# SwiGLU's token groups in the order second, third, first, with the first group's products by seven for eight

## The chip, the cores and the metric

The kernel runs on one core of a Trainium2 chip. The metric is the time of one execution on the device in microseconds; of several runs the median counts. The profile is one further execution, recorded by the hardware profiler, with its own time.

## What is computed

Attention with softmax on q (over the head dimension) and on k (over the sequence), an expert layer in which every expert is applied to all 2304 tokens and weighted by a matrix P (eight rounds of row and column normalization), and a SwiGLU layer with an RMS norm ahead of it:

```python
x = attn_out.transpose(0, 2, 1, 3).reshape(2304, 512)
# experts: P from exp(x @ w_gate), 8 rounds
for e in range(8):
    out += P[:, e:e + 1] * (np.maximum(x @ w1[e], 0.0) @ w2[e])   # 512 -> 1024 -> 512
# SwiGLU on x = out
xn = x / sqrt(mean(x * x) + 1e-06) * rms_g
g = xn @ w_gate                                                  # 512 -> 1536
return (g * sigmoid(g) * (xn @ w_val)) @ w_out
```

## The kernel before

**Precision.** Every operand of a large product is split into a high and a low part (`split`, L100); `mm3` (L104) issues three matmuls for one product: high by high, high by low, low by high. In the trace these are lines 105, 106 and 107.

**Groups and units.** The tokens are in three groups of 512, 896 and 896 tokens; `GP` (L55) holds half of these, 256, 448 and 448. Features of the hidden layers are taken 256 at a time (`CH`). One such chunk for one group is a unit: 32 units a group in the expert layer (units 0 to 95, `NU` is 96), six a group in SwiGLU (`NC2` is 6, units 96 to 113). Each unit has a part h, which computes the hidden features, and a part y, which multiplies them with the second weights and adds to the group's sum, one 128-token tile after another: four tiles in group 0, seven in the others, six matmuls of 512 columns for each tile.

**Two ways of h.** `plain` (L845) multiplies directly: 24 matmuls of 512 columns for group 0. `seven` (L793) takes the product as two by two blocks and makes it from seven block products instead of eight (`PROD`, L788): 42 matmuls whose columns are one half of the group's tokens, 448. It needs sums and differences of the weight blocks (stored to DRAM ahead, loaded by `ws_load`, L287) and of the token blocks (seven tiles `SX`, named B11, T1, B21, T2, B22, T4, T3, built in 36 steps by `sx_all`, stored in DRAM, loaded by `sx_load`, L739). The seven products go to three PSUM places b1, b2, b3, of which b1 alone has two buffers. After each product something reads it out: ScalarE copies (`keep`, L800, line 802 in the trace) after products 1, 2, 4 and 7, VectorE adds after 3, 5 and 7 (lines 816, 820, 825), GpSimd adds after 7 (line 826). Group 0 goes by `plain` in both layers, the others by `seven`.

**SwiGLU.** `unit2_h` (L1040) makes the gate product a, applies the sigmoid on ScalarE (L1046) and multiplies on VectorE (L1047), then makes the value product v, multiplies (L1050), and splits the result for y (L1052, L1053). In the groups by seven the a pass and the v pass follow each other directly: 84 matmuls. The second weights are split in task places 4 and 5 of the a pass (`w2_split`), after which the next ones are requested.

**Order.** `stretch` (L1141) writes out the order of the parts on TensorE: within a stretch h of the next unit comes ahead of y of the unit before, and a new stretch begins with h, h, y. Three calls make: expert groups 0 and 1; expert group 2 with SwiGLU groups 0 and 1; SwiGLU group 2. The side work is hung by `task` and `spread` (L1242) on numbered places within h and y, one step a place; each engine runs its instructions in the order issued. All transfers are issued by SyncE (SP) in order. `norm_steps` (L1029) makes the RMS norm of a group: sums of squares on ScalarE (L953), a root (L957), scaling on VectorE (L974), transposes on TensorE with copies on ScalarE (L1020), and the `sx_all` steps. For group 0 it ends instead in `norm_first` (L978), which stores the normed tokens in `XN0D`; `first_again` (L996) loads them for SwiGLU.

Of the kernel before, what the change touches and what calls it, by code (L numbers as in the profile page):

```python
# [8 lines left out]
F32 = mybir.dt.float32  # L9
# [9 lines left out]
def kernel(  # L19
# [23 lines left out]
    nc = tc.nc  # L43
# [26 lines left out]
    EPS = 1e-9  # L70
    LATE = 4

    const = ctx.enter_context(tc.tile_pool(name="const", bufs=1))
# [213 lines left out]
    def ws_load(key):  # L287

        ws_alloc(key)
        for w, t in zip("hl", WS[key]):  # L290
            t = t.rearrange("p a k f -> p (a k f)").bitcast(F32)
            if key[1] < NU:
                nc.sync.dma_start(t, WSD[key + (w,)])
            else:
                g, c = divmod(key[1] - NU, NC2)
                d = WSD[key[0], c, w]
                if g:
                    nc.sync.dma_start(t, d[:, 2 * P:])
                else:
                    nc.sync.dma_start(t[:, :8 * P], d[:, :8 * P])  # L300

# [434 lines left out]
    def sx_alloc(nm, g):  # L736
        SX[nm] = sxp.tile([P, 2, 2, G], F32R, tag=nm, name=f"s{nm}_{g}")

    def sx_load(g, i):  # L739
        nm = NAMES[i]  # L740
        sx_alloc(nm, g)
        nc.sync.dma_start(SX[nm].rearrange("p w j n -> p (w j n)").bitcast(F32), SXD[nm, g])

    def sx_steps(g, j, b11, b21, b12, b22, stored):

        shp = b11.shape[1:]

        v = (lambda t: t.rearrange("p (a n) -> p a n", a=shp[0])) if len(shp) > 1 \
            else (lambda t: t)

        def put(nm, s):
            if stored:
                if j == 0:
                    SXD[nm, g] = dram.tile(
                        [P, 4 * G], F32, tag=f"{nm}{g}", name=f"sd{nm}_{g}"
                    )
                d = SXD[nm, g].rearrange("p (w j n) -> p w j n", w=2, j=2)
                return list(halves(
                    f"{nm}_{g}_{j}", s, lambda t: v(t[:, :G]), lambda w: v(d[:, w, j]),
                    None if g == NG + 2 else staged,  # L760
                ))
# [15 lines left out]

# [15 lines left out]
    def seven(key, c, hook, after):  # L793

        wh, wl = WS.pop(key)
        nm = f"{key[0]}_{key[1]}"
        bk = {}
        tmp = {}

        def keep(n, i):  # L800
            tmp[n] = cp_.tile([P, G], F32, tag="u1" if n == "u3" else n, name=f"{n}_{nm}")
            nc.scalar.copy(tmp[n], bk[i])  # L802

        for i, (w, x, b, first) in enumerate(PROD):
            if first:
                bk[b] = pb_tile(f"b{b}", f"b{b}_{nm}_{i}")[:, :G]
            s = SX[x]
# [25 lines left out]
    def group(u):  # L833
        return (u // NCH, u % NCH) if u < NU else divmod(u - NU, NC2)

# [8 lines left out]

    def plain(u, f, key, stored):  # L845

        ph = bank("h", 2 * GP[0], f"ph_{key[0]}_{u}_{f}")
        plain_mm(ph, f, key, stored, range(KD))
        return ph

    def plain_mm(ph, f, key, stored, kks):
        wh, wl = WS[key]
        xh, xl = X0
        for kk in kks:
            if stored:
                i = ((2, 3), (0, 1))[f][kk // 2]
                lh, ll = wh[:, i, kk % 2], wl[:, i, kk % 2]
            else:
                lh, ll = (plain_view(t)[:, kk, f * P:(f + 1) * P] for t in (wh, wl))
            mm3(ph, lh, ll, xh[:, kk], xl[:, kk], kk == 0, kk == KD - 1)  # L860
# [9 lines left out]
    def unit_h(u, hook):  # L870
        if u < NCH:
            hook(0)
            for f in range(2):
                if f:
                    hook(1)
                if u == 0:
                    ph = FIRST_PH[f]
                    plain_mm(ph, f, ("a", 0), False, (KD - 1,))
                else:
                    ph = plain(u, f, ("a", u), False)  # L880
                relu(*h_tiles(u, f), ph)()
            del WS["a", u]
            hook(2)
            return
# [90 lines left out]

    XN0D = {}

    def norm_first(kk):  # L978

        pn = bank("y", DM, f"pn_0_{kk}")  # L980
        for t in range(TPG[0]):
            nc.tensor.transpose(
                pn[:, t * P:(t + 1) * P], ACC[0, 0][:, t, kk * P:(kk + 1) * P], ident
            )
        hi, lo = piece(f"xn0_{kk}")
        nc.scalar.activation(hi, pn, AF.Copy, scale=rmsg[:, kk:kk + 1])
        nc.vector.scalar_tensor_tensor(
            lo, pn, rmsg[:, kk:kk + 1], hi.bitcast(F32), op0=ALU.mult, op1=ALU.subtract
        )
        if kk == 0:  # L990
            XN0D[0] = dram.tile([P, 2 * KD * DM], F32, tag="xn0", name="xn0")
        d = XN0D[0].rearrange("p (w k n) -> p w k n", w=2, k=KD)
        for w, t in enumerate((hi, lo)):
            nc.sync.dma_start(d[:, w, kk], t.bitcast(F32))

    def first_again():  # L996
        nonlocal X0
        t = slot_a()
        nc.sync.dma_start(t.bitcast(F32), XN0D[0])
        X0 = as_x0(t)  # L1000

    def norm_place(g, kk, h):
# [3 lines left out]
    def norm_transpose(g, kk):  # L1006
        n = TPG[g]
        per = P // 2
        pns = []
        for i in range(2):  # L1010
            pn = bank("y", DM, f"pn_{g}_{kk}_{i}")
# [12 lines left out]

        out_(0, 0, n, pns[0][:, :n * per])
        out_(1, 0, 8 - n, pns[0][:, n * per:])
# [13 lines left out]
    def unit2_h(u, hook):  # L1040
# [15 lines left out]

        cg = cp_.tile([P, 2, 2, G], F32, tag="c", name=f"cg_{u}")
        if g == 0:
            for f in range(2):
                hook(f)  # L1060
                to = cg[:, f].rearrange("p t g -> p (t g)")[:, :n]
                gate_part(plain(u, f, ("a", u), True), to, f)
            del WS["a", u]
            hook(2)
            for f in range(2):
                hook(3 + f)
                to = cg[:, f].rearrange("p t g -> p (t g)")[:, :n]
                value_part(plain(u, f, ("v", u), True), to, f)()
            del WS["v", u]
            hook(5)  # L1070
            return
        flat = lambda t, f: t[:, f].rearrange("p t g -> p (t g)")
        cv = cp2.tile([P, 2, 2, G], F32, tag="cv", name=f"cv_{u}")
        hook(-1)
# [72 lines left out]
    stretch(0, 2 * NCH)  # L1147
    stretch(2 * NCH, NCH + 2 * NC2)
    stretch(NU + 2 * NC2, NC2)

# [27 lines left out]
    for n, key in enumerate(keys):  # L1178
# [4 lines left out]
        i = 6 if kd == "a" else 13  # L1183
        if u >= NU and group(u)[0] == 0:
            i = 2 if kd == "a" else 5
        task("h", u, i, lambda key=key: ws_load(key))
# [101 lines left out]
    for i in range(7):  # L1288
        task("h", NU + 2 * NC2 - 1, 7 + i, lambda i=i: sx_load(NG + 2, i))

    with tc.manual_schedule():
# [52 lines left out]
        def first_h(i):  # L1344
            if i == 0:
                FIRST_PH.extend(bank("h", 2 * GP[0], f"ph_a_0_{f}") for f in range(2))
            for f in range(2):
                plain_mm(FIRST_PH[f], f, ("a", 0), False, (i,))

# [147 lines left out]
```

## Time and profile before

| | |
|---|---|
| median of 3 runs | 2025.71 us (2025.29 to 2025.9) |
| the profiled execution | 2025.36 us, span 2023.6 us |
| TensorE busy | 1999.9 us, 99% |
| VectorE busy | 1408.3 us, 70% |
| ScalarE busy | 782.7 us, 39% |
| GpSimd busy | 412.5 us, 20% |
| DMA | 415.09 MB, mean 205 GB/s |
| share of TensorE in the chain that ended last | 95% |

Busy time of TensorE counts a matmul from its start to its modelled end; consecutive matmuls overlap in the records, so the rate of work is read from the number of matmuls in a stretch, not from the mean duration of one. Idle time of an engine that is not the bottleneck costs nothing.

### The profile page before, as it was taken

To read this page: it belongs to the slowest core of one execution; us is meant where nothing else is said; L and a number is where in the kernel's file an instruction comes from. 1 tells how busy PE (TensorE), PEld (TensorE's weight loads), DVE (VectorE), ACT (ScalarE), POOL (GpSimd) and SP (SyncE) were. 2 spreads that over 40 slices of the span, in tenths; PEclk is the share of its full clock that TensorE was granted. 3 is DMA by queue.
4 is the path that set the end of the run, shared out by engine and by line. 5 is a ranking of instruction groups with operands and counts; after the bars stand their busy time and mean duration, and the time that the engine had idled before them with its cause. 6 is when DMAs were issued, how large, how long until landed. Compare 5 with 4: busy or idle time off the path is not lost.

```text
span 2023.6 us, 25473 instructions
## 1 busy us (share of the span) xinstructions
PE 1999.9 (99%) x9454; PEld 1727.4 (85%) x9454; DVE 1408.3 (70%) x2161; ACT 782.7 (39%) x1383; POOL 412.5 (20%) x388
## 2 busy tenths in 40 slices
PE   7999999999999999999999999999999999999999
PEld 5887888888888888888888888888888888888887
DVE  8785877776767777777658878878865446565555
ACT  5554333345433434433243333333332243432432
POOL 5551000031222222222013222222220000110100
PEclk9999999999999999999999999999999999999999
DMA  7443223355755566554777778878865647657542
GB/s 205 132 138 105 94 95 99 99 186 183 263 202 203 210 220 219 205 201 176 292 268 267 258 246 313 278 264 291 281 235 189 263 144 262 217 203 271 195 159 75
DMA packets 154236, 415.09 MB, mean 205 GB/s; under 512 B 13568, under 2 KB 66304, under 8 KB 153728
## 3 DMA queue, kind: packets, MB, share of 16 engines
q1 hardware_dynamic: 154112, 413.47, 58.6%
q8 instruction: 74, 1.21, 0.2%
q14 instruction: 50, 0.41, 0.1%
HBM read 281.69 MB, written 131.73 MB: 204 GB/s over the span
## 4 chain that ended last, share of the span: by engine, by line
PE 95%; DVE 3%; DMA 1%; ACT 0%; issue 0%; POOL 0%; SPq 0%; DVEq 0%; POOLq 0%; ACTq 0%
PE py L105 13%; PE py L106 13%; PE py L107 13%; PE b_a L107 10%; PE b_a L106 10%; PE b_a L105 10%; PE ph_a L105 3%; PE ph_a L107 3%; PE ph_a L106 3%; PE po L107 2%; PE po L105 2%; PE po L106 2%; PE b_v L105 2%; PE b_v L107 2%; PE b_v L106 2%; PE pv L573 1%
## 5 line engine op out<-in xcount | busy, mean ns | idle before, releaser
L105 PE MATMUL py<-w2h,hh 128*128 128x512 f32 x1152 | 452.7, 393 | 0.7 <-ACT lt L685 0.7
L106 PE MATMUL py<-w2l,hh 128*128 128x512 f32 x1152 | 449.0, 390 | 0.0
L107 PE MATMUL py<-w2h,hl 128*128 128x512 f32 x1152 | 448.6, 389 | 0.0
L802 ACT COPY u_a<-b_a 128x448 f32<-128x448 f32 x228 | 121.6, 533 | 693.6 <-PE b_a L107 693.4
L105 PEld LDWEIGHTS py<-w2h,hh 128*128 128x128 f32 x1152 | 216.2, 188 | 47.2 <-issue 1.5
L107 PEld LDWEIGHTS py<-w2h,hl 128*128 128x128 f32 x1152 | 216.3, 188 | 45.7
L106 PEld LDWEIGHTS py<-w2l,hh 128*128 128x128 f32 x1152 | 216.4, 188 | 43.0
L105 PE MATMUL b_a<-sT,wsh_a 128*128 128x448 f32 x608 | 220.1, 362 | 3.3 <-DVE c L816 2.1
L107 PE MATMUL b_a<-sT,wsl_a 128*128 128x448 f32 x608 | 220.7, 363 | 0.0
L106 PE MATMUL b_a<-sT,wsh_a 128*128 128x448 f32 x608 | 220.3, 362 | 0.0
L930 DVE SCALAR_TENSOR_TENSOR slot_a<-py,Pm,slot_a 128x512 f32<-128x512 f32 x217 | 162.5, 749 | 52.4 <-PE py L107 50.3
L930 DVE SCALAR_TENSOR_TENSOR slot_b<-py,Pm,slot_b 128x512 f32<-128x512 f32 x217 | 161.1, 745 | 23.5 <-PE py L107 22.5
L107 PE MATMUL b_a<-sB,wsl_a 128*128 128x448 f32 x456 | 165.7, 363 | 0.1
L106 PE MATMUL b_a<-sB,wsh_a 128*128 128x448 f32 x456 | 165.2, 362 | 0.0
L105 PE MATMUL b_a<-sB,wsh_a 128*128 128x448 f32 x456 | 165.2, 362 | 0.0
L102 DVE TENSOR_TENSOR w2l<-w2r,w2h 128x512 fp32r<-128x512 f32 x162 | 118.2, 730 | 43.6 <-ACT w2h L101 43.6
L826 POOL TENSOR_TENSOR c<-u_a,p_a 128x448 f32<-128x448 f32 x64 | 73.9, 1155 | 344.3 <-ACT u_a L802 344.2
L864 DVE SCALAR_TENSOR_TENSOR hl<-c,hh 128x896 fp32r<-128x896 f32 x128 | 143.1, 1118 | 0.9 <-ACT hh L863 0.7
L247 POOL TENSOR_TENSOR sum<-w1r 128x256 f32<-128x256 f32 x32 | 23.7, 741 | 562.2 <-DMA w1r<-in_moe_w_dram 244.2
L863 ACT ACTIVATE hh<-c 128x896 fp32r<-128x896 f32 x128 | 122.3, 956 | 27.9 <-POOL c L826 27.9
L101 ACT CAST w2h<-w2r 128x512 fp32r<-128x512 f32 x162 | 97.1, 618 | 81.4 <-PE py L107 77.0
L105 PEld LDWEIGHTS b_a<-sT,wsh_a 128*128 128x128 f32 x608 | 113.7, 187 | 13.2 <-DVE c L816 3.7
(236 smaller groups left out, 3654.6 us busy)
## 6 DMA issues: line engine op xcount, KB each, us to landing
w2r<-in_moe_w_dram SPq DMA_DIRECT2D x96, 512.0 KB, 4.6
w1r<-in_moe_w_dram SPq DMA_DIRECT2D x64, 512.0 KB, 3.4
wsdh<-wsh_a SPq DMA_DIRECT2D x32, 896.0 KB, 6.6
wsdl<-wsl_a SPq DMA_DIRECT2D x32, 896.0 KB, 7.9
wsh_a<-wsdh SPq DMA_DIRECT2D x32, 896.0 KB, 6.5
wsl_a<-wsdl SPq DMA_DIRECT2D x32, 896.0 KB, 8.5
w2d<-w2l SPq DMA_DIRECT2D x32, 512.0 KB, 2.9
w2l<-w2d SPq DMA_DIRECT2D x32, 512.0 KB, 4.8
```

Of the source, the lines that this page charges most:

```text
L101: nc.scalar.copy(hi, src)
L102: (eng or nc.vector).tensor_tensor(lo, src, hi.bitcast(F32), op=ALU.subtract)
L105: nc.tensor.matmul(ps, lh, rh, start=first, stop=False, skip_group_check=True)
L106: nc.tensor.matmul(ps, lh, rl, start=False, stop=False, skip_group_check=True)
L107: nc.tensor.matmul(ps, ll, rh, start=False, stop=last, skip_group_check=True)
L247: nc.gpsimd.tensor_tensor(s1, a21, a22, op=ALU.add)
L573: nc.tensor.matmul(st["pv"][:, :P], st["ke"][:, c].rearrange("p h d -> p (h d)"), st["v"][:, :, c, :], start=(c == 0), stop=(c == SC - 1),)
L802: nc.scalar.copy(tmp[n], bk[i])
L826: nc.gpsimd.tensor_tensor(c[:, 1, 1], tmp["u3"], tmp["p5"], op=ALU.add)
L863: nc.scalar.activation(th, src, AF.Relu)
L864: return lambda: nc.vector.scalar_tensor_tensor(tl, src, 0.0, th.bitcast(F32), op0=ALU.max, op1=ALU.subtract)
L930: nc.vector.scalar_tensor_tensor(a, py, pe, a, op0=ALU.mult, op1=ALU.add)
```

## The change

SwiGLU's groups come in the order 1, 2, 0 (`TURN2`), and each has a stretch of its own. Group 0's unit goes by `seven` as the others', with block columns of 256 tokens, so an h of SwiGLU has 84 matmuls in every group. Group 0's norm ends in transposes and the 36 `sx_all` steps, with DRAM tiles of its own; `norm_first`, `XN0D` and `first_again` go. The norm of group 0 has more places (units 33 to 38, h and y), the `sx_all` of expert group 2 begins two units later, the norm of group 2 lies in five units of SwiGLU group 1 (ten places in h, three in y), and the SX tiles of the three groups are loaded during the last h of the group ahead of each. Weight blocks are loaded at the same places in all groups: 14 of 16 blocks for group 0 too, where it had 8.

```diff
+    TURN2 = (1, 2, 0)
 def ws_load(key):
-                if g:
-                    nc.sync.dma_start(t, d[:, 2 * P:])
-                else:
-                    nc.sync.dma_start(t[:, :8 * P], d[:, :8 * P])
+                nc.sync.dma_start(t, d[:, 2 * P:])
 def sx_alloc(nm, g):
-        SX[nm] = sxp.tile([P, 2, 2, G], F32R, tag=nm, name=f"s{nm}_{g}")
+        w = GP[g % NG]
+        t = sxp.tile([P, 4 * G], F32R, tag=nm, name=f"s{nm}_{g}")[:, :4 * w]
+        SX[nm] = t.rearrange("p (w j n) -> p w j n", w=2, j=2)
 def seven(key, c, hook, after):
+        w_ = GP[group(key[1])[0]]
-                bk[b] = pb_tile(f"b{b}", f"b{b}_{nm}_{i}")[:, :G]
+                bk[b] = pb_tile(f"b{b}", f"b{b}_{nm}_{i}")[:, :w_]
 def group(u):
+        j, c = divmod(u - NU, NC2)
+        return TURN2[j], c
 def norm_steps(g):
-        if g == 0:
-            return steps + [lambda kk=kk: norm_first(kk) for kk in range(KD)]
 def unit2_h(u, hook):
-        if g == 0:
-            for f in range(2):
-                hook(f)
-                gate_part(plain(u, f, ("a", u), True), to, f)
-            for f in range(2):
-                hook(3 + f)
-                value_part(plain(u, f, ("v", u), True), to, f)()
-            return
 ...
-    stretch(2 * NCH, NCH + 2 * NC2)
-    stretch(NU + 2 * NC2, NC2)
+    stretch(2 * NCH, NCH)
+    for j in range(NG):
+        stretch(NU + j * NC2, NC2)
 ...
-            task("h", u, (0 if group(u)[0] == 0 else 4) + f, lambda u=u, f=f: w2_split(u, f))
+            task("h", u, 4 + f, lambda u=u, f=f: w2_split(u, f))
-    spread([("h", u, i) for u in range(34, 38) for i in (0, 1, 3, 4)], lambda: norm_steps(0))
+    spread(
+        [at for u in range(33, 39) for at in
+         [("h", u, i) for i in (0, 1, 3, 4)] + [("y", u - 1, i) for i in range(6)]][6:],
+        lambda: norm_steps(0),
+    )
-        [("y", u, i) for u in range(39, 57) for i in (3, 5)],
+        [("y", u, i) for u in range(41, 59) for i in (3, 5)],
-    task("y", NU - 3, 0, first_again)
-        task("h", NU, 0, lambda i=i: sx_load(NG + 1, i))
+        task("h", NU - 1, i, lambda i=i: sx_load(NG + 1, i))
+        task("h", NU + NC2 - 1, 7 + i, lambda i=i: sx_load(NG + 2, i))
+        task("h", NU + 2 * NC2 - 1, 7 + i, lambda i=i: sx_load(NG, i))
     spread(
-        [("y", NU + i // 4, i % 4) for i in range(12)]
-        + [("h", NU + 3 + i // 5, i % 5) for i in range(15)]
-        + [("h", u, i) for u in range(NU + NC2, NU + 2 * NC2 - 1) for i in (0, 1, 3, 4, 7, 9)],
+        [at for u in range(NU, NU + NC2 - 1) for at in
+         [("h", u, i) for i in (0, 1, 2, 3, 4, 7, 8, 9, 10, 11)]
+         + [("y", u - 1, i) for i in (1, 3, 5) if u > NU]],
         lambda: norm_steps(2),
     )
```

## Rows read from the trace of the kernel before

**Rows 1.** The page: busy us (share of the span) and instructions.

```profile
PE 1999.9 (99%) x9454; PEld 1727.4 (85%) x9454; DVE 1408.3 (70%) x2161; ACT 782.7 (39%) x1383; POOL 412.5 (20%) x388
```

**Rows 2.** Stretches: start:end us, length, TensorE busy us, matmuls, clock, DMA share, GB/s.

```profile
483.64:493.52 9.88, 8.70 (x44) 1.00 0.29 99
...
1618.93:1635.25 16.32, 16.32 (x74) 1.00 0.52 163
1692.82:1701.22 8.40, 8.40 (x43) 1.00 0.40 160
1701.22:1709.82 8.60, 8.60 (x43) 1.00 0.75 240
...
1874.73:1884.96 10.23, 8.95 (x43) 1.00 0.49 180
```

**Rows 3.** Small matmuls: time order (start, us, count); groups (busy us, mean ns).

```profile
104.80 1.06 PE L573 MATMUL pv<-v,ke 96*128 96x128 f32 x8
166.22 1.62 PE L693 MATMUL pt<-sel,lt 128*128 128x8 f32 x14
L573 PEld LDWEIGHTS pv<-v,ke x192: 186/192/337, 10.6 to 174.0; 96*128 96x128 f32 x192
...
L105 PEld LDWEIGHTS b_a<-sT,wsh_a 128*128 128x128 f32 x608 | 113.7, 187 | 13.2 <-DVE c L816 3.7 <-ACT u_a L802 1.5
```

**Rows 4.** Time order where v follows a, group 2: start, us, instruction, wait.

```profile
1991.26 0.36 PE L105 MATMUL b_v<-sB,wsh_v 128*128 128x448 f32 x1
1991.52 0.54 ACT L802 COPY u_a<-b_a 128x448 f32<-128x448 f32 x1 [0.27 <-PE b_a L107]
1991.79 0.68 DVE L102 TENSOR_TENSOR w2l<-w2r,w2h 128x512 fp32r<-128x512 f32 x1
1992.18 1.30 POOL L826 TENSOR_TENSOR cg<-u_a,p_a 128x448 f32<-128x448 f32 x1 [16.13 <-ACT u_a L802]
1993.52 0.95 ACT L1046 ACTIVATE sg<-cg 128x896 f32<-128x896 f32 x1 [1.47 <-POOL cg L826]
1994.38 0.51 ACT L802 COPY u_v<-b_v 128x448 f32<-128x448 f32 x1
...
1994.94 0.47 PE L105 MATMUL b_v<-sT,wsh_v 128*128 128x448 f32 x1
```

**Rows 5.** Groups by shape: the readers' work at 256 and 512 columns.

```profile
L650 ACT CAST slot_a<-px 128x256 fp32r<-128x256 f32 x8 | 2.7, 375 | 0.8 <-PE px L635 0.7
L1046 ACT ACTIVATE sg<-ph_a 128x512 f32<-128x512 f32 x12 | 7.2, 598 | 15.8 <-PE ph_a L107 15.8
L101 ACT CAST w2h<-w2r 128x512 fp32r<-128x512 f32 x36 | 22.1, 613 | 19.1 <-PE py L107 15.0 <-PE po L107 4.1
L657 DVE TENSOR_TENSOR slot_a<-px,slot_a 128x256 fp32r<-128x256 f32 x8 | 2.9, 408 | 0.8 <-ACT slot_b L652 0.8
L1047 DVE TENSOR_TENSOR cg<-ph_a,sg 128x512 f32<-128x512 f32 x12 | 8.3, 691 | 16.9 <-ACT sg L1046 16.9
L248 POOL TENSOR_TENSOR sum<-w1r 128x256 f32<-128x256 f32 x32 | 36.3, 1135 | 0.0
L247 POOL TENSOR_TENSOR sum<-w1r 128x256 f32<-128x256 f32 x32 | 23.7, 741 | 562.2 <-DMA w1r<-in_moe_w_dram 244.2 <-issue 194.3 <-ACT p_a L802 108.2
```

**Rows 6.** Time order at the border into SwiGLU group 2.

```profile
1867.36 0.34 SPq L186 DMA_DIRECT2D w2r<-w  x1
1868.27 0.38 SPq L298 DMA_DIRECT2D wsl_a<-wdl_a  x1
...
1875.42 0.47 PE L107 MATMUL b_a<-sB,wsl_a 128*128 128x448 f32 x1
```

**Rows 7.** The norm's work by groups; last row: TensorE's waits, 480 to 530 us.

```profile
L953 ACT ACTIVATE pch_junk<-slot_b 128x512 f32<-128x512 f32 x7 | 4.4, 630 | 0.0
L1046 ACT ACT_TABLE_LOAD x2 | 2.6, 1283 | 0.0
L953 ACT ACTIVATION_READ_ACCUMULATOR pch_junk<-slot_b 128x1 f32 x7 | 1.3, 190 | 0.0
PE b_a L105 <- DVE c L816: 1.2, 1, 1.2
```

More of the change, by code (lines that the diff above doesn't have):

```diff
@@ L294, in ws_load @@
             else:
-                g, c = divmod(key[1] - NU, NC2)
+                c = (key[1] - NU) % NC2
                 d = WSD[key[0], c, w]
-                if g:
-                    nc.sync.dma_start(t, d[:, 2 * P:])
-                else:
-                    nc.sync.dma_start(t[:, :8 * P], d[:, :8 * P])
+                nc.sync.dma_start(t, d[:, 2 * P:])
     DN = KD * CH // 2
@@ L736, in sx_alloc @@
     def sx_alloc(nm, g):
-        SX[nm] = sxp.tile([P, 2, 2, G], F32R, tag=nm, name=f"s{nm}_{g}")
+        w = GP[g % NG]
+        t = sxp.tile([P, 4 * G], F32R, tag=nm, name=f"s{nm}_{g}")[:, :4 * w]
+        SX[nm] = t.rearrange("p (w j n) -> p w j n", w=2, j=2)
+        return t
     def sx_load(g, i):
         nm = NAMES[i]
-        sx_alloc(nm, g)
-        nc.sync.dma_start(SX[nm].rearrange("p w j n -> p (w j n)").bitcast(F32), SXD[nm, g])
+        nc.sync.dma_start(sx_alloc(nm, g).bitcast(F32), SXD[nm, g])
     def sx_steps(g, j, b11, b21, b12, b22, stored):
         shp = b11.shape[1:]
+        n = GP[g % NG]
         v = (lambda t: t.rearrange("p (a n) -> p a n", a=shp[0])) if len(shp) > 1 \
@@ L754, in put @@
                     SXD[nm, g] = dram.tile(
-                        [P, 4 * G], F32, tag=f"{nm}{g}", name=f"sd{nm}_{g}"
+                        [P, 4 * n], F32, tag=f"{nm}{g}", name=f"sd{nm}_{g}"
                     )
@@ L758, in put @@
                 return list(halves(
-                    f"{nm}_{g}_{j}", s, lambda t: v(t[:, :G]), lambda w: v(d[:, w, j]),
-                    None if g == NG + 2 else staged,
+                    f"{nm}_{g}_{j}", s, lambda t: v(t[:, :n]), lambda w: v(d[:, w, j]),
+                    None if g in (NG, NG + 2) else staged,
                 ))
@@ L800, in keep @@
         def keep(n, i):
-            tmp[n] = cp_.tile([P, G], F32, tag="u1" if n == "u3" else n, name=f"{n}_{nm}")
+            tmp[n] = cp_.tile(
+                [P, G], F32, tag="u1" if n == "u3" else n, name=f"{n}_{nm}"
+            )[:, :w_]
             nc.scalar.copy(tmp[n], bk[i])
@@ L833, in group @@
     def group(u):
-        return (u // NCH, u % NCH) if u < NU else divmod(u - NU, NC2)
+        if u < NU:
+            return divmod(u, NCH)
+        j, c = divmod(u - NU, NC2)
+        return TURN2[j], c
     def h_tiles(u, f):
@@ L843, in h_tiles, with plain, plain_mm @@
         return t
-    def plain(u, f, key, stored):
+    def plain(u, f, key):
         ph = bank("h", 2 * GP[0], f"ph_{key[0]}_{u}_{f}")
-        plain_mm(ph, f, key, stored, range(KD))
+        plain_mm(ph, f, key, range(KD))
         return ph
-    def plain_mm(ph, f, key, stored, kks):
+    def plain_mm(ph, f, key, kks):
         wh, wl = WS[key]
@@ L854, in plain_mm @@
         for kk in kks:
[L855 to L859, printed above, removed]
+            lh, ll = (plain_view(t)[:, kk, f * P:(f + 1) * P] for t in (wh, wl))
             mm3(ph, lh, ll, xh[:, kk], xl[:, kk], kk == 0, kk == KD - 1)
@@ L877, in unit_h @@
                     ph = FIRST_PH[f]
-                    plain_mm(ph, f, ("a", 0), False, (KD - 1,))
+                    plain_mm(ph, f, ("a", 0), (KD - 1,))
                 else:
-                    ph = plain(u, f, ("a", u), False)
+                    ph = plain(u, f, ("a", u))
                 relu(*h_tiles(u, f), ph)()
@@ L974, in norm_scale @@
         nc.vector.tensor_scalar_mul(a, a, SS[g][:, t:t + 1])
[L976 to L1000, printed above, removed]
     def norm_place(g, kk, h):
@@ L1009, in norm_transpose @@
         pns = []
-        for i in range(2):
+        for i in range(1 if g == 0 else 2):
             pn = bank("y", DM, f"pn_{g}_{kk}_{i}")
@@ L1025, in norm_transpose @@
         out_(0, 0, n, pns[0][:, :n * per])
+        if g == 0:
+            out_(1, 0, n, pns[0][:, n * per:])
+            return
         out_(1, 0, 8 - n, pns[0][:, n * per:])
@@ L1055, in value_part @@
             )
-        cg = cp_.tile([P, 2, 2, G], F32, tag="c", name=f"cg_{u}")
-        if g == 0:
-            for f in range(2):
-                hook(f)
-                to = cg[:, f].rearrange("p t g -> p (t g)")[:, :n]
-                gate_part(plain(u, f, ("a", u), True), to, f)
-            del WS["a", u]
-            hook(2)
-            for f in range(2):
-                hook(3 + f)
-                to = cg[:, f].rearrange("p t g -> p (t g)")[:, :n]
-                value_part(plain(u, f, ("v", u), True), to, f)()
-            del WS["v", u]
-            hook(5)
-            return
+        w = GP[g]
+        four = lambda t: t.rearrange("p f t g -> p (f t g)")[:, :4 * w].rearrange(
+            "p (f t g) -> p f t g", f=2, t=2
+        )
         flat = lambda t, f: t[:, f].rearrange("p t g -> p (t g)")
-        cv = cp2.tile([P, 2, 2, G], F32, tag="cv", name=f"cv_{u}")
+        cg = four(cp_.tile([P, 2, 2, G], F32, tag="c", name=f"cg_{u}"))
+        cv = four(cp2.tile([P, 2, 2, G], F32, tag="cv", name=f"cv_{u}"))
         hook(-1)
@@ L1183 @@
         i = 6 if kd == "a" else 13
-        if u >= NU and group(u)[0] == 0:
-            i = 2 if kd == "a" else 5
         task("h", u, i, lambda key=key: ws_load(key))
@@ L1260 @@
     )
-    spread([("h", u, i) for u in range(34, 38) for i in (0, 1, 3, 4)], lambda: norm_steps(0))
+    spread(
+        [at for u in range(33, 39) for at in
+         [("h", u, i) for i in (0, 1, 3, 4)] + [("y", u - 1, i) for i in range(6)]][6:],
+        lambda: norm_steps(0),
+    )
     def third():
@@ L1278 @@
     )
-    task("y", NU - 3, 0, first_again)
     for i in range(7):
-        task("h", NU, 0, lambda i=i: sx_load(NG + 1, i))
+        task("h", NU - 1, i, lambda i=i: sx_load(NG + 1, i))
+        task("h", NU + NC2 - 1, 7 + i, lambda i=i: sx_load(NG + 2, i))
+        task("h", NU + 2 * NC2 - 1, 7 + i, lambda i=i: sx_load(NG, i))
     spread(
-        [("y", NU + i // 4, i % 4) for i in range(12)]
-        + [("h", NU + 3 + i // 5, i % 5) for i in range(15)]
-        + [("h", u, i) for u in range(NU + NC2, NU + 2 * NC2 - 1) for i in (0, 1, 3, 4, 7, 9)],
+        [at for u in range(NU, NU + NC2 - 1) for at in
+         [("h", u, i) for i in (0, 1, 2, 3, 4, 7, 8, 9, 10, 11)]
+         + [("y", u - 1, i) for i in (1, 3, 5) if u > NU]],
         lambda: norm_steps(2),
     )
-    for i in range(7):
-        task("h", NU + 2 * NC2 - 1, 7 + i, lambda i=i: sx_load(NG + 2, i))
     with tc.manual_schedule():
@@ L1347, in first_h @@
             for f in range(2):
-                plain_mm(FIRST_PH[f], f, ("a", 0), False, (i,))
+                plain_mm(FIRST_PH[f], f, ("a", 0), (i,))
         WOPS = dict(wl=loads, w1=first_w1, w2=first_w2, H=first_h)
```

## The prediction

> **What bounds the kernel now.** I read the busy times first: TensorE is busy 1999.9 of 2023.6 us [rows 1], so time can only come from fewer or shorter matmuls, and be lost only where TensorE waits. The second view is the busy time of exact stretches, cut at unit borders [rows 2]. It gives the pitch of one matmul, start to start. Three plain passes of group 0 are 72 matmuls of 512 columns in 16.32 us: 226.7 ns each (the row counts 74, because neighbours reach in at the edges). Products by seven for 448 columns: 42 matmuls in 8.40 us, 200.0 ns. From these two the slope is 26.7 / 64 = 0.417 ns a column and the rest 13.3 ns. The same view shows where TensorE waits: 0.2 us in each v pass that follows an a pass (8.60 against 8.40), 1.8 us in the a pass that follows a v pass with no y between (10.23), 1.5 us in one pass of the expert stage (9.88). Everything else runs at the pitch, so the question is what the change does to the columns and what it does to these waits.
>
> **Term 1, the products of group 0.** Before, one unit's a and v passes are 48 matmuls at 226.7 ns, 10.88 us. After, they are 84 matmuls of 256 columns. No matmul of this type and width is in the trace. The line through the two measured widths gives 13.3 + 256 x 0.417 = 120 ns. From below, the k-v products of attention have 128 columns and a new weight load for each matmul; eight take 1.06 us including a last one of 0.275, a pitch of 112 ns, and the tiny gate matmuls with 8 columns, which can only be held by their weight loads, go at about 105 ns [rows 3]. From above, a weight load is recorded as 187 to 192 ns; if that were its price in a stream, the pitch would be 190. It is not: the k-v loads of that recorded length follow each other at 112 [rows 3]. I take 120, since it comes from the same type and the same loads, and keep 112 and 130. So 84 x 0.120 = 10.08 us, a gain of 0.80 a unit, **-4.8 us** for six (at 112: -8.8; at 130: about 0).
>
> The Trainium skill (TensorE: Matmul & The Clock Gate, section Back-to-back issue gap) has the gap at columns / 2.4 + 2.5 ns, 109 ns for 256. The trace differs at both widths it has, 226.7 against the rule's 216 and 200.0 against 189, so the measurement decides; by the rule term 1 would be -10.3 us, and the sum would still be slower.
>
> **Term 2, the wait between a and v in group 0.** The time order at 448 columns shows the wait, from T0, the first v matmul (1991.26) [rows 4]. The last product of a ends; ScalarE copies u3 from +0.26 for 0.54; GpSimd adds for 1.30; the sigmoid runs 0.95; only then does ScalarE copy v's first product, and the fourth product, which writes the same bank again, starts at +3.68 where three products take 3.60. At 256 columns three products take only 2.16. The parts [rows 5]: a copy 0.375, a sigmoid of 512 columns 0.60, the GpSimd add between 0.74 and 1.13, take 0.85. ScalarE also has the second w2 cast (0.61, task 5) in front, which the shorter pass pulls up against the copy: the second add of c ends at T0 - 0.77, the first sigmoid at -0.12, the cast at +0.49, so the copy ends at +0.83, GpSimd at 1.80, the sigmoid at 2.44, the next copy at 2.73, and TensorE starts at 2.78. That is 0.62 late, part of which already falls at the third product, which waits for VectorE's last add behind w2's subtract. Six units: **+3.7 us** (GpSimd at its two ends: 3 to 5.4). The group's y passes stay at 24 matmuls of 512.
>
> **Term 3, the border into group 0.** Each group now begins a stretch of its own: h, h, y. The second unit's a weights are requested when the first unit's a pass is read out, but on SP's queue behind the next w2 load, which waits for w2's subtract. In the border of before, the w2 load goes at T0 + 1.23, the two weight loads right behind, and the matmul that first needs the low half starts at 1875.42, 8.06 us later [rows 6]. The 448-column v pass (8.60) covered nearly all of that. At 256 columns the v pass takes 5.04 + 0.62, and the subtract ends at T0 + 1.28, so the third matmul of the next a pass starts at 1.31 + 8.06 = 9.37 instead of 5.90: **+3.5 us** (2.5 to 4.5). The ScalarE chain at that border is hidden under it. In the steady state the y pass (5.44) lies between: 11.3 us for the same 9.4, no wait. The v weights of the second unit come just in time.
>
> **Term 4, the border into group 1.** Before, the order ran on from group 0 into group 1 with y between. Now the first two units of group 1 are back to back at full width; this is the case measured at the border into group 2, 10.23 against 8.40: **+1.8 us**. Group 2 keeps its own. The group's SX loads move from the cover of group 0 into the last expert unit and two y passes; the same loads at the earlier expert border fit there, so I cost them at nothing; if late, up to 2.
>
> **Term 5, the norm of group 2.** Its 55 steps stood partly in group 0, which left ScalarE slack; now all lie in five units of group 1, ten of thirteen places a unit inside products. In the first unit five sums of squares (0.63 each) and the first sigmoid's table load (1.28) fall into the a pass [rows 7]. ScalarE then has four copies 2.13, sums 3.15, casts 1.22, load 1.28, sigmoid 0.95 = 8.7 us from +1.46 on, and ends 1.0 late (with the read-out of 0.19 a sum, 1.9): take 1.2. The root's chain ScalarE-VectorE stops VectorE in the middle of products; at its only place of that kind before, the norm of group 0, TensorE lost 1.2 us in one wait and 1.5 in the pass [rows 2, 7]: 1.5. In the second unit the sigmoid's table is loaded again, 1.28 with 0.3 of slack: 1.0. Four transposes at consecutive products need ScalarE copies of 1.5 us each beside 0.5 of the pass's own in 1.9 us: 1.0. Together **+4.7 us**; at the lower end, if ScalarE catches up, 2, at the upper 9.
>
> **Terms at nothing.** The norm of group 0 gains 36 steps of about 0.4 us in expert units where TensorE never waits on the y side; its root stays in a product pass, so its 1.5 us stays. XN0D's stores and reload go; they bounded nothing. The end has the same add and stores.
>
> **Sum.** -4.8 + 3.7 + 3.5 + 1.8 + 4.7 = +8.9. The profiled execution took 2025.36 us, 0.35 below the median shown, so 2034.3, in the runs' terms about **2034**. A measurement tells 0.2%, 4 us, from no change.
>
> **Rivals.** (a) Not slower: the norm finds cover. Place: ScalarE in the first two units of group 1. If its backlog drains in the y passes before a bank is wanted, term 5 falls to 0 and, with a pitch of 112, terms 1 and 2 are -8.8 + 4.9, so -8.8 + 4.9 + 3.5 + 1.8 = +1.4: 2027. It decides at a ScalarE delay under 0.3 us. For it: ScalarE is busy 39% [rows 1]; against: the passes of these two units have more ScalarE work than time. Same, 0.20. Faster needs, besides, that the border weights come early and a-v waits stay at 0.2: -8.8 + 1.2 + 0 + 1.8 = -5.8, 2020: 0.06. (b) The weight load's recorded 190 ns is the pitch: 84 x 0.19 - 10.88 = 5.1 a unit, +30 with no a-v wait: about 2064. For: every load row. Against: the small matmuls [rows 3]. 0.05. (c) Weights are late in every unit of group 0: a unit now loads about 4.2 MB in 16 us instead of 2.6, and the margin is 2 us; 4 us late in five units is +20: 2054. 0.04. My own case has 0.65.
>
> **How the numbers follow.** Slower: my case, (b), (c): 0.74; same 0.20; faster 0.06. Range: term 1 at 112 with small waits gives 2025 to 2026; term 1 at 130 with the upper ends of terms 3 and 5 gives 2043. So 2025 to 2044.
>
> **What would show it.** 84 matmuls in 10.1 us a unit; the fourth product of v 0.6 late, in six units; a single gap of 3 to 4 us at group 0's second unit with the low weights as releaser; 1.8 us plus a ragged first two units in group 1. Wrong if the pitch is 190, if group 0's gaps recur in each unit, or if group 1 shows no more than its 1.8.

## The result and the profile after

The changed kernel took 2036.31 us (median of four, 2033.89 to 2040.35), against 2025.55 for the kernel before: ratio 1.0055, interval 1.0041 to 1.0068. It is slower, by 11 us where 9 were forecast. The profiled execution took 2036.0 us.

The page's busy times, which answer [rows 1]:

```profile
span 2034.1 us, 26172 instructions
PE 2001.8 (98%) x9670; PEld 1735.6 (85%) x9670; DVE 1427.3 (70%) x2215; ACT 802.4 (39%) x1449; POOL 425.5 (21%) x400
```

There are 216 matmuls more, as 36 a unit in six units must give: the change does what it says. Busy time rose by 2 us and the span by 10.5, so most of the loss is in waits, although busy time also holds matmuls that ran at a lower clock, as the next view shows. It has stretches of the changed kernel, cut at pass borders, as in [rows 2] (start:end, length, TensorE busy, matmuls, clock, DMA share, GB/s); an a pass is the gate product of one unit, a v pass the value product behind it:

```profile
466.30:475.17 8.87, 8.69 (x44) 1.00 0.14 50
475.17:487.36 12.19, 11.64 (x60) 1.00 0.54 202
1605.14:1617.28 12.14, 10.27 (x43) 0.86 0.52 194
1609.50:1614.00 4.50, 4.42 (x14) 0.62 0.92 320
1617.28:1628.29 11.01, 8.96 (x44) 1.00 0.47 168
1628.29:1639.81 11.52, 11.52 (x72) 1.00 0.53 205
1932.18:1939.46 7.28, 5.65 (x44) 1.00 0.68 251
1939.46:1947.78 8.32, 6.64 (x43) 0.79 0.74 286
1941.50:1944.00 2.50, 2.37 (x11) 0.50 0.96 384
1959.08:1964.03 4.95, 4.95 (x43) 1.00 0.43 177
1964.03:1969.81 5.78, 5.49 (x44) 1.00 0.61 204
```

In the order of the sum: the two stretches at 1959 and 1964 are an a and a v pass of group 0, 42 matmuls in 4.95 us, 117.9 ns each, and 0.83 more where v follows a. Those at 1932 and 1939 are the border into group 0: the first unit's v pass is 1.50 longer than the later ones, the second unit's a pass 3.37 longer. Those at 1605, 1617 and 1628 are the first two units of group 1: the first v pass takes 12.14 against the usual 8.60, the second a pass 11.01 against 8.41, and the second v pass 11.52, with 28 transposes of group 2's norm in it. The border into group 2 takes 10.24 as before. The first two rows are the root of group 0's norm in the expert stage, 8.87 where 9.88 stood, and a y pass with that norm's transposes.

Before, the transposes of group 2's norm stood in a y pass and an a pass of group 0, which took 14.05 us together instead of 10.88, 3.17 more:

```profile
1651.57:1665.62 14.05, 14.05 (x78) 1.00 0.28 80
```

What TensorE waited for, in group 0 and then in the first units of group 1 (us in total, times, longest):

```profile
PE b_a L108 <- DMA wsl_a<-wdl_a: 1.7, 1, 1.7
PE b_a L106 <- DMA wsh_a<-wdh_a: 1.3, 1, 1.3
PE b_v L106 <- ACT u_v L806: 1.2, 6, 0.2
...
PE b_v L106 <- DVE cg L829: 1.9, 1, 1.9
PE b_a L106 <- ACT u_a L806: 1.5, 1, 1.5
PE b_a L106 <- DVE cv L829: 0.5, 1, 0.5
```

The border into group 0 waits for weights, high and low halves; v's wait recurs six times, for ScalarE's copy; group 1 waits twice for VectorE's last add (line 829 is 825 of before), once for a copy.

How the first of group 1's waits arises, in time order (rows between these are left out):

```profile
1604.04 1.28 ACT L1023 ACT_TABLE_LOAD   x1
1605.33 0.95 ACT L1023 ACTIVATE sg<-cg 128x896 f32<-128x896 f32 x1
1606.32 1.09 DVE L1024 TENSOR_TENSOR cg<-cg,sg 128x896 f32<-128x896 f32 x1 [2.09 <-ACT sg L1023]
1607.31 1.13 POOL L830 TENSOR_TENSOR cg<-u_a,p_a 128x448 f32<-128x448 f32 x1 [27.68 <-ACT u_a L806]
1607.33 1.66 DVE L103 TENSOR_TENSOR w2l<-w2r,w2h 128x512 fp32r<-128x512 f32 x1
1608.91 0.61 DVE L829 TENSOR_TENSOR cg<-b_a,u_a 128x448 f32<-128x448 f32 x1
...
1609.58 0.47 PE L106 MATMUL b_v<-sB,wsh_v 128*128 128x448 f32 x1 [1.88 <-DVE cg L829]
```

The table load starts at 1604.04, when ScalarE has worked off five sums of squares. VectorE idles 2.09 us for the sigmoid, then has the multiplication and w2's subtract to do before the add that frees bank b2, and TensorE stands until 1609.58. The 4.5 us from there on run at 0.62 of the full clock on average.

### The profile page after: what moved, and what is told of

It reads as the page before. It is cut to its first block, busy times and chain, and to the rows that moved or that the text cites. A ratio compares the mean times of both kernels' runs of the same rounds, so it can differ in the third digit from the quotient of the medians.

```text
span 2034.1 us, 26172 instructions
## 1 busy us (share of the span) xinstructions
PE 2001.8 (98%) x9670; PEld 1735.6 (85%) x9670; DVE 1427.3 (70%) x2215; ACT 802.4 (39%) x1449; POOL 425.5 (21%) x400
## 4 chain that ended last, share of the span: by engine, by line
PE 93%; DVE 3%; ACT 2%; issue 1%; DMA 1%; POOL 1%; SPq 0%; DVEq 0%; POOLq 0%; ACTq 0%
PE py L106 13%; PE py L107 13%; PE py L108 13%; PE b_a L108 11%; PE b_a L106 10%; PE b_a L107 10%; PE ph_a L106 3%; PE ph_a L108 3%; PE ph_a L107 3%; PE po L106 2%; PE po L107 2%; PE po L108 2%; PE b_v L106 2%; PE b_v L108 2%; PE b_v L107 2%; PE pv L571 1%
## 5 line engine op out<-in xcount | busy, mean ns | idle before, releaser
L806 ACT COPY u_a<-b_a 128x448 f32<-128x448 f32 (+1 forms) x246 | 128.3, 521 | 715.9 <-PE b_a L108 713.0
L106 PE MATMUL b_a<-sT,wsh_a 128*128 128x448 f32 (+1 forms) x656 | 233.8, 356 | 3.8 <-ACT u_a L806 2.7
L108 PE MATMUL b_a<-sT,wsl_a 128*128 128x448 f32 (+1 forms) x656 | 234.3, 357 | 0.0
L107 PE MATMUL b_a<-sT,wsh_a 128*128 128x448 f32 (+1 forms) x656 | 234.0, 357 | 0.0
L108 PE MATMUL b_a<-sB,wsl_a 128*128 128x448 f32 (+1 forms) x492 | 176.3, 358 | 1.8 <-DMA wsl_a<-wdl_a 1.7
L106 PE MATMUL b_a<-sB,wsh_a 128*128 128x448 f32 (+1 forms) x492 | 175.7, 357 | 1.9 <-DMA wsh_a<-wdh_a 1.3
L107 PE MATMUL b_a<-sB,wsh_a 128*128 128x448 f32 (+1 forms) x492 | 175.6, 357 | 0.0
L106 PEld LDWEIGHTS b_a<-sT,wsh_a 128*128 128x128 f32 x656 | 123.0, 188 | 14.1 <-ACT u_a L806 3.4
L107 PEld LDWEIGHTS b_a<-sT,wsh_a 128*128 128x128 f32 x656 | 123.4, 188 | 8.7
```

The lines of the kernel that those rows point to most:

```text
L106: nc.tensor.matmul(ps, lh, rh, start=first, stop=False, skip_group_check=True)
L107: nc.tensor.matmul(ps, lh, rl, start=False, stop=False, skip_group_check=True)
L108: nc.tensor.matmul(ps, ll, rh, start=False, stop=last, skip_group_check=True)
```

## The experiments

Each run is the changed kernel with the edit shown, unless it says otherwise. Times are medians of 4 to 11 executions, and each ratio stands against the kernel before.

### e1: the sums and the root of group 2's norm in the last expert y

```diff
-        [at for u in range(NU, NU + NC2 - 1) for at in
+        [("y", NU - 1, i) for i in (0, 1, 2, 3, 4, 5, 6, 6)]
+        + [at for u in range(NU, NU + NC2 - 1) for at in
          [("h", u, i) for i in (0, 1, 2, 3, 4, 7, 8, 9, 10, 11)]
```

> The changed kernel with one edit: the seven sums of squares and the root of group 2's norm move from the first two passes of SwiGLU group 1 into the last y of the expert layer, tile by tile, where ScalarE is idle. Theory: the waits of group 1's first unit (its v pass 12.15 us against 8.60, the next a pass 11.01 against 10.23) come from ScalarE's sums and the sigmoid's table load ahead of the copies, which hold VectorE and with it bank b2. Then the v pass comes to 8.6 to 9.0 and the a pass to 10.2 to 10.5, and the time falls by 3.5 to 4.5 us to about 2032. Rival: these waits belong to the border itself (SX tiles loaded late, two h back to back); then the v pass stays at about 12 us and the time at 2036.

Measured: 2043.1 us, ratio 1.0085 (1.0070 to 1.0100). Slower, where a gain was expected; at the border itself the gain came. Stretches: the first v pass and the second a pass at the border, then two y passes of group 1.

```profile
1604.92:1617.63 12.71, 11.46 (x64) 1.00 0.49 186
1617.63:1627.62 9.99, 9.73 (x50) 1.00 0.72 254
1662.84:1678.54 15.70, 11.58 (x43) 0.89 0.69 241
1695.55:1709.35 13.80, 11.61 (x43) 0.88 0.64 257
```

The border passes now contain the transposes (64 and 50 matmuls instead of some 43). Without these, 3.07 us in the first and 0.68 in the second, they take 9.6 and 9.3: most of the waits went, as the theory has it, though the v pass stays 1.0 over its usual 8.60. But two y passes of 9.6 became 15.7 and 13.8. The edit pulled all later steps eight places ahead. In the view of waits around these two:

```profile
ACT pch_B L385 <- DMA sdT<-pch_T: 5.4, 1, 5.4
```

ScalarE waits 5.4 us for a store of token pieces to leave one of the two piece buffers; a store had been issued right behind two weight loads of 0.9 MB each, and what stood behind the piece in ScalarE's and VectorE's order, the readers of y's banks among it, waited as well. Whether moving the sums or moving the rest did this is not told by this run alone; e5 tells it.

### e2: groups 2 and 0 in one stretch

```diff
-    for j in range(NG):
-        stretch(NU + j * NC2, NC2)
+    stretch(NU, NC2)
+    stretch(NU + NC2, 2 * NC2)
```

> The changed kernel with one edit: SwiGLU groups 2 and 0 in one stretch, so that y of group 2's last unit stands between the first and second h of group 0. Theory: the 4.9 us lost at group 0's second unit (1.5 at the high weights, 1.9 at the low ones, the rest matmuls at half clock behind the wait) come from the request time of the second unit's weights, which have only a v pass of 5 us to land in; with 9.5 us of y between they are there, and the time falls by 4 to 5 us to about 2032. The SX tiles of group 0 then have one y pass instead of two to land in; if they are late, up to 2 us come back at the first unit. Rival: the transfers are short of bandwidth; then the weights of the next units are late in turn, and the time falls by less than 1.5 us.

Measured: 2030.7 us, ratio 1.0027 (1.0016 to 1.0037), 5.6 less than the changed kernel. First unit of group 0 (a, v), second unit (a):

```profile
1918.86:1924.39 5.53, 5.19 (x43) 1.00 0.70 284
1924.39:1929.80 5.41, 5.22 (x44) 1.00 0.72 246
1939.36:1944.31 4.95, 4.95 (x43) 1.00 0.78 233
```

No weight is late, in the second unit or in any later one, and 0.6 us is paid at the first unit for one token tile. So the border's cost was the request time, with too little work behind it, and not the bandwidth, and this run's rival falls. The prediction's rival (c), weights late in every unit, had fallen with the changed kernel's own waits, which name weights at one border alone.

### e3: the second sigmoid behind v's second copy

```diff
                 keep("p5", 3)
+                while DEFER:
+                    DEFER.pop(0)()
...
-        seven(("a", u), cg, hook, lambda f: gate_part(flat(cg, f), flat(cg, f), f))
+        seven(("a", u), cg, hook, gated)      # gated(1) appends to DEFER
```

> The changed kernel with one edit: the a pass's second sigmoid and its multiplication are issued behind v's second product copy instead of ahead of its first. Theory: the wait of v's fourth product (in group 0's six units some 0.45 us of the 0.82 us by which a v pass is longer than an a pass; in the twelve other units 0.18) is ScalarE's order, the copy standing behind a sigmoid that waits for GpSimd. It goes; the third product's wait for VectorE (0.34) stays. The time falls by 3 to 5 us to about 2032. The copy still shares its buffer with GpSimd's input, so some 0.1 may stay at the fourth product and some at the fifth. Rival: the fourth product waits for its weights or tokens; then nothing changes.

Measured: 2034.71 us, ratio 1.0042 (1.0027 to 1.0057): 1.6 less than the changed kernel, half of what was expected at least, and the runs of the two overlap (2033.17 to 2035.35 here, 2033.89 to 2040.35 there), so the passes tell more than the time. A v pass of 448 columns, then an a and a v pass of group 0:

```profile
1711.69:1720.11 8.42, 8.42 (x44) 1.00 0.72 232
1958.07:1963.02 4.95, 4.95 (x44) 1.00 0.39 160
1963.02:1968.77 5.75, 5.47 (x44) 1.00 0.62 220
```

and TensorE's waits in five units of group 0, 0.2 us each as in the changed kernel, where the releaser was ScalarE's copy:

```profile
PE b_v L106 <- DVE cv L824: 1.0, 5, 0.2
```

At 448 columns the 0.18 is gone. At 256 the wait has the same length, but stands at the sixth product and not at the fourth, and has another releaser: the multiplication, moved along with the sigmoid, now stands ahead of VectorE's add (line 824) that frees the sixth product's bank. The wait at the third product stays, as expected. The theory named the wait rightly and its cure wrongly: not the copy's place alone, but the whole chain has to fit into what narrow products leave.

### e4: group 0 by the plain product, in the new order

```diff
     def unit2_h(u, hook):
+        if g == 0:
+            for f in range(2):
+                hook(f)
+                gate_part(plain(u, f, ("a", u), True), to, f)
...
+    task("y", NU + 2 * NC2 - 2, 0, first_again)
-        task("h", NU + 2 * NC2 - 1, 7 + i, lambda i=i: sx_load(NG, i))
```

> The changed kernel with group 0 by the plain product again (8 of 16 weight blocks, normed tokens stored and reloaded as before), in the new order 1, 2, 0. It tells the order from the products. Theory: products by seven gain 5.9 us (4.95 against 5.44 us a pass, twelve passes) and lose 5.0 in v's waits and 4.9 at the border, so without them the time is 4 us lower, about 2032, and the order alone with the moved norm costs 6 to 7 us over the kernel before, all of it in group 1's first two units. Rival one: the narrow products are the whole loss; then 2025 to 2027. Rival two: the order is the whole loss and the products are a gain; then 2039 to 2042.

Measured: 2033.49 us, ratio 1.0038 (1.0024 to 1.0052): 2.8 under the changed kernel, 7.7 over the kernel before. First v pass and second a pass at group 1's border; the second unit's a pass in group 0:

```profile
1604.80:1615.63 10.83, 8.96 (x44) 1.00 0.54 206
1615.63:1627.95 12.32, 9.23 (x43) 1.00 0.44 161
1937.61:1944.03 6.42, 5.78 (x26) 1.00 0.55 169
```

TensorE's longest wait in the first of them, as long as in the changed kernel:

```profile
PE b_v L106 <- DVE cg L832: 1.9, 1, 1.9
```

Both single causes fall. The narrow products are not the whole loss, since 7.7 us stay without them. The order is not the whole either: the medians' 2.8 us is within the spread of the runs, but in the traces the a and v passes of group 0 take 4.0 us more than before in the changed kernel and 1.0 here. The loss at group 1's border (10.83 and 12.32, the same sum as 12.14 and 11.01) is there with group 0 plain, so it is the order's and the norm's. The 1.0 is the border into group 0 (6.42 against 5.44), with 8 of 16 weight blocks to load and longer passes to load them in.

### e5: e1 with the later steps at their places

```diff
+        [("y", NU - 1, i) for i in (0, 1, 2, 3, 4, 5, 6, 6)]
+        + [at for u in range(NU, NU + NC2 - 1) for at in
+           [("h", u, i) for i in (0, 1, 2, 3, 4, 7, 8, 9, 10, 11)]
+           + [("y", u - 1, i) for i in (1, 3, 5) if u > NU]][8:],
```

> As e1, but every step from group 2's third scale on keeps the place that it has in the changed kernel, so that only the sums, the root and two scales move (the places left free stay empty). In e1 the border waits went (v pass 9.6, a pass 9.3 with transposes, 4.4 us less) but two y passes of group 1 lost 6.1 and 4.2 us. Theory: those came from the shifted places alone: a store of token pieces fell right behind two weight loads, so ScalarE waited 5.4 us for a free piece, and VectorE and the y pass with it; with the places of the changed kernel they go, the border gain stays, and the time is 4 to 5 us under the changed kernel, about 2032. Rival: moving sums and root earlier itself brings these waits (piece buffers held by the sums' outputs); then the time stays above 2036.

Measured: 2032.16 us, ratio 1.0033 (1.0021 to 1.0046). Border passes, and the y pass that took 15.70 in e1:

```profile
1604.81:1614.40 9.59, 8.93 (x43) 1.00 0.63 232
1614.40:1624.90 10.50, 8.95 (x43) 1.00 0.53 189
1663.04:1672.95 9.91, 9.87 (x43) 1.00 0.89 353
```

12.14 and 11.01 became 9.59 and 10.50, 3.1 us less, 4.1 in the medians, and the y pass is near the 9.88 that it takes in the changed kernel. So e1's loss was the shift of places alone. The edit moves eight steps, the seven sums and the root; the two scales that the expectation names keep their places. About half of the 3.1 is clock: these passes run at 1.00, the changed kernel's 12.14 at 0.86. The v pass stays 1.0 over its usual 8.60, so the sums and the root are not the whole loss there.

### e6: multiplication behind v's third add, half of w2's split in the v pass

```diff
                 nc.vector.tensor_tensor(c[:, 0, 0], bk[2], tmp["u1"], op=ALU.add)
+                while DEFER:
+                    DEFER.pop(0)()
...
-            task("h", u, 4 + f, lambda u=u, f=f: w2_split(u, f))
+            task("h", u, 4 + 7 * f, lambda u=u, f=f: w2_split(u, f))
```

> The changed kernel with two edits in SwiGLU's products: the a pass's second sigmoid and its multiplication are issued behind v's third add (in e3, behind v's second copy), and the second half of the w2 split moves from the a pass (place 5) to the v pass (place 11). In e3 the wait did not go but moved in group 0: from the fourth product (ScalarE's copy) to the sixth, whose bank is freed by VectorE's add that then stood behind the multiplication, 0.34 us; at 448 columns there was room and the 0.18 went. Theory: with the add ahead of the multiplication and w2's subtract out of the way of the a pass's last add, both waits of group 0's v pass go: 5.77 to at most 5.1, six times, some 4.5 us, and 0.18 in each of the other units, 2 us. The border into group 0 also gains, since the w2 load no longer stands ahead of the second unit's weights: its 4.9 falls to 1.5 to 3.5. The time: 2026 to 2029. Rival: the chain through GpSimd is as long as three narrow products in any order; then the waits turn up at another product and the time falls by no more than 2 to 3 us.

Measured: 2037.14 us, ratio 1.0057 (1.0042 to 1.0073), as slow as the changed kernel, where a gain was expected. A v pass of group 0; a y pass of group 1; second unit of group 0 (a, v):

```profile
1968.50:1973.45 4.95, 4.95 (x45) 1.00 0.77 277
...
1666.93:1677.44 10.51, 10.08 (x43) 1.00 0.84 298
1940.06:1947.36 7.30, 5.59 (x44) 1.00 0.95 359
1947.36:1958.07 10.71, 7.85 (x42) 0.68 0.52 197
```

The v pass of group 0 is down to 4.95, as long as an a pass: not a trace of the wait, so the chain does fit in another order, and the rival falls. Three costs outweigh that. In the wide groups y grew to between 9.95 and 10.5 us, TensorE waiting for VectorE's adds among others (line 1076, up to 0.4 us each). The border into group 0 costs 8.1 us instead of 4.9, where a gain was expected: with the v pass shorter still and the w2 load now ahead of the second unit's v weights, those are late too (2.9 us for the low half), and that pass runs at 0.68 of the full clock on average. And the two passes at group 1's border take 24.0 us together instead of 23.2.

### e7: e2, e5 and e6 together

The edits of e2, e5 and e6, and this one for two h back to back:

```diff
                 keep("p5", 3)
+                while LAST:
+                    LAST.pop(0)()()
...
-            fn = value_part(flat(cv, f), flat(cg, f), f)
             if f:
-                NEXT.append(fn)
+                LAST.append(lambda: value_part(flat(cv, f), flat(cg, f), f))
```

> e2, e5 and e6 together, and the v pass's second value product issued behind the next a pass's second copy where two h stand back to back. If the losses of the changed kernel are the separate terms that the runs name, they add: 5.6 of e2, 4.5 of e5, 6 of e6 (its share at the border is already e2's) and about 1 at each of the two borders left, so 2018 to 2021, under the kernel before by 0.2 to 0.4%. If they share a cause or cover each other, the sum falls short: 2024 to 2028.

Measured: 2023.52 us, ratio 0.9992 (0.9983 to 1.0000). Under the kernel before by 1.8 us, with an interval that reaches no change, and 3 to 5 us short of the sum; e6 had already shown the missing part, the y passes of the wide groups.

### e8: e7 with w2's split moved in group 0 alone

```diff
-            task("h", u, 4 + 7 * f, lambda u=u, f=f: w2_split(u, f))
+            at_ = 4 + f if group(u)[0] else 4 + 7 * f
+            task("h", u, at_, lambda u=u, f=f: w2_split(u, f))
```

> e7 with one edit: the second half of the w2 split goes to the v pass in group 0 alone; in groups 1 and 2 it stays in the a pass. In e6 and e7 the wide groups' y passes of 9.6 us became 9.95 to 10.5 (TensorE at the fifth and sixth tile waiting for a bank that VectorE reads out), 10 to 11 of them. Theory: the subtract and the multiplication that moved into the v pass leave VectorE behind at the start of y; with w2 back in the a pass half of that load goes and y falls back to 9.6: 4 us less than e7, 2019 to 2021. Rival: the moved multiplication is enough to make the y passes late; then the time stays at 2022 to 2024.

Measured: 2019.34 us, ratio 0.9970 (0.9958 to 0.9981), 17 under the changed kernel and 6.2 under the kernel before. A y pass of group 2 and the first a pass of group 0:

```profile
1821.48:1831.03 9.55, 9.55 (x44) 1.00 0.58 204
1910.14:1915.85 5.71, 5.16 (x44) 1.00 0.71 290
```

The y pass is back at its usual length, and the later a and v passes of group 0 take 4.95 each. So the terms add, to about 17 us, once each of them is taken out where it stands.

### e9: the kernel before with the moved sigmoid and value product

The sigmoid and multiplication moved as in e6 (behind the third add) and the value product as in e7, in the kernel before; w2's split keeps its places.

> The kernel before with the two moves that do not need the change: the second sigmoid behind v's third add, the second value product behind the next a pass's second copy. It tells how much of e8 is the change's. Theory: 0.18 in each of twelve v passes and about 0.5 at the one border, 2 to 3 us: 2022.5 to 2024, so that the change itself, with its waits taken out, is worth 2 to 4 us. Rival: the moves bring y waits here too; then 2025 to 2027, no gain.

Measured: 2022.49 us, ratio 0.9985 (0.9976 to 0.9994). So 3.0 of e8's 6.2 us are to be had without the change, and about 3.2 are its own.

### e10: e8 with group 0 by the plain product

The edits of e4 on e8.

> e8 with group 0 by the plain product (weights and tokens as in e4), all else equal: the order 1, 2, 0, the joined border, the early sums and the moved sigmoid and value product. It measures what products by seven with 256 columns are worth where nothing waits behind them. Theory: twelve passes of 4.95 instead of 5.44 us are worth 5.9 us and the waits at their borders are equal within 1, so this kernel takes 5 to 6.5 us more than e8, 2024 to 2026. Rival: part of the gain is given back elsewhere (longer transfers, VectorE, the clock), so that the plain product takes no more than 3 us more.

Measured: 2025.84 us, ratio 1.0002 (0.9993 to 1.0011), 6.5 more than e8. In its trace a plain pass takes 5.44 us as before, and 1.4 is paid at the border, where TensorE waits 1.1 us for the reloaded tokens. e8 pays 0.7 at the same border, so the 6.5 are the 5.9 us of the count and some 0.7 of the border. The new order with its third border and the moved norm takes back about 3 of what e9 has (2025.84 against 2022.49); which of these takes it was not tried.

## Why the prediction was right

It forecast 2034, 2025 to 2044, slower with 0.74; the time is 2036.3. The mechanisms it named are those that the traces show, each at its place; their sizes are partly off, and the total is nearer than they are. By its steps:

**Term 1, -4.8.** Measured 4.95 against 5.44 in twelve passes, -5.9. The line through two widths gave 120 ns, the matmuls take 117.9. Rival (b), 190 ns, is out: the weight load's recorded length, 188 ns here, is not its price in a stream. The Trainium skill's rule (TensorE: Matmul & The Clock Gate, section Back-to-back issue gap) gives 109 ns and is short here as it was at the other widths.

**Term 2, +3.7.** The chain is as it was told, but v passes are 0.83 longer than a passes, where 0.62 a unit was forecast, 5.0 in all:

```profile
1964.40 0.36 ACT L806 COPY u_a<-b_a 128x256 f32<-128x256 f32 x1
1964.89 1.01 POOL L830 TENSOR_TENSOR cg<-u_a,p_a 128x256 f32<-128x256 f32 x1 [9.30 <-ACT u_a L806]
1965.22 0.42 DVE L829 TENSOR_TENSOR cg<-b_a,u_a 128x256 f32<-128x256 f32 x1
1965.69 0.39 PE L106 MATMUL b_v<-sB,wsh_v 128*128 128x256 f32 x1
1965.93 0.63 ACT L1023 ACTIVATE sg<-cg 128x512 f32<-128x512 f32 x1 [1.17 <-POOL cg L830]
1966.47 0.35 ACT L806 COPY u_v<-b_v 128x256 f32<-128x256 f32 x1
1966.87 0.39 PE L106 MATMUL b_v<-sT,wsh_v 128*128 128x256 f32 x1 [0.21 <-ACT u_v L806]
```

The copy ends 0.73 after v's first matmul (1964.03), GpSimd at 1.87, the next copy at 2.79, and TensorE starts at 2.84 where 2.78 was forecast. So the chain's end was right to 0.06, because two errors nearly cancel: GpSimd's add takes 1.01 us, where 0.85 was taken from a range of 0.74 to 1.13, and the copy ahead of it ends 0.10 earlier. The rest of the 0.21 a unit is that three products take 2.12 and not 2.16, and that the first matmul after the fourth product's wait holds the next one back 0.11 longer than in a stream (1966.87 to 1967.10). Some 0.35 of the 0.83 falls at the third product (1965.69), for VectorE's last add, as the prediction said. e6 shows the cause: with the sigmoid and w2's subtract out of the order, the wait is zero. There GpSimd's add takes 0.74:

```profile
1969.26 0.74 POOL L834 TENSOR_TENSOR cg<-u_a,p_a 128x256 f32<-128x256 f32 x1 [8.73 <-DVE cg L1028]
```

In e6 w2's subtract no longer runs beside it. That the subtract is what makes it 1.01 is not shown.

**Term 3, +3.5.** Measured 4.9. The wait for the weights is 3.4 of it, from start to start (1.5 at the high half, 1.9 at the low), as sized; e2 and the view of waits show it. The rest, 1.5, was not in the sum: the matmuls after the wait ran at half clock.

**Terms 4 and 5, +1.8 and +4.7.** Measured 3.5 in the first unit's v pass, 2.6 in the second's a pass and 0.3 in a y pass; the second's v pass, with the transposes, is 2.9 over its usual 8.60, which is 0.2 less than the transposes cost before. That is 6.2 against 6.5, and the total agrees better than its parts. The sums and the table load cost 3.5, not 1.2: the delay went through VectorE's order to bank b2, which was costed for ScalarE alone, and 1.6 of it is clock again. If term 4's 1.8 is taken as forecast, the root, the second table load and the transposes cost 0.9 instead of 3.5; how the second a pass divides between them was not tried. That the sums and the root are a cause is shown by e5 (3.1 us of the 6.1 that the first two of these passes lose), that group 0's products are not by e4.

**Terms at nothing.** The norm of group 0 gained 0.7 us in the expert stage instead of none: its root, at another place, makes a pass of 8.87 instead of 9.88, less 0.3 that the passes with its transposes and behind them take more. The time up to the end of the expert layer, SwiGLU's products left out, fell by 0.4.

The sum of the measured terms is -5.9 + 5.0 + 4.9 + 6.2 - 0.4 = +9.8, against 10.5 between the two spans. The other 0.7 lies in y passes that the sum had as unchanged: 0.4 in group 2's first (9.95 against 9.59), 0.3 in group 0's (5.48 against 5.44) and behind the last. Their cause was not looked for.

That the total came out so near is in part luck. The half clock, which no term has, took 1.5 us at the border into group 0 and 1.6 in group 1; without these 3.1 the sum of the same passes would be 7.4, an estimate, since terms 1, 4 and 5 came out lower than forecast by 3.0 and term 2 higher by 1.3. Rival (a) was near in kind: once the norm has most of its cover (e5) the changed kernel is still slower, because terms 2 and 3 stay; only all of them together turn the sign.

## What to carry to other kernels

A transformation that saves multiplications by making products narrower also shortens the cover of every chain and every transfer that ran behind a product: 0.5 us a pass was saved here, and 0.8 in every second pass lost to a chain that was late by only 0.2 at 448 columns, so the chains are to be recomputed at the new width first. A step that is moved within an in-order engine takes its wait along: name the next consumer on each engine it passes (e3, e6), and keep later steps at their places (e1 against e5 is 11 us). And where a group of work begins, ask what was requested ahead of it and what runs while it lands: a border without other work between costs what the passes there do not cover of the transfer, 3.4 us here.

## What the runs showed of the hardware

- The granted clock halved after waits of TensorE of 1.9 and 3.0 us: 0.50 from 1941.5 to 1944.0 after 3.0 us of waits in two parts, 0.62 on average from 1609.5 to 1614.0 after one wait of 1.9. In e4 the same wait of 1.9 for VectorE at the same place (10.83 us pass, granted clock 1.00) did not lower it. So it doesn't follow each time, and costs about 1.5 us where it does. Why it follows in one run and not in the other is open. The four runs of the changed kernel go with their mean granted clocks: 2033.89 us at 1.000, 2036.00 and 2036.62 at 0.998, 2040.35 at 0.996. The Trainium skill (TensorE: Matmul & The Clock Gate, section What's actually happening) has two levels of the clock, 1.2 and 2.4 GHz. The rows of 0.50 and 1.00 agree with these.
- A subtract of 512 columns on VectorE took 1.66 us beside a GpSimd addition that started 0.02 us ahead of it at 1607.31, where it takes 0.68 in the rows of before [rows 4]. This is one case, and its cause was not tried.
- A float32r matmul of 256 columns, with a new weight load for each, has a pitch of 117.9 ns, though its weight load is recorded with 188.
